# A recurrent attention with two expert layers on one core: low parts of the weights on VectorE, bounded scans, bonus sums on TensorE, and a new order of the slots

## The chip, the core and the metric

The kernel runs on 1 core of one Trainium2 chip. The metric is the device time of one execution in microseconds (us); lower is better.

## The reference

```python
for t in range(S):                                   # B, H, S, D = 4, 8, 768, 48
    cur = np.einsum('bhd,bhe->bhde', u[None] * kt, vt)
    y[:, :, t] = np.einsum('bhd,bhde->bhe', rt, state + cur)
    state = wt[:, :, :, None] * state + np.einsum('bhd,bhe->bhde', kt, vt)
x = y as (B * S, H * D)                              # 3072 tokens, 384 channels
gate = 1 / (1 + exp(-(x @ w_gate)));  val = x @ w_val   # 384 -> 1536
x = gate * val @ w_out                                  # 1536 -> 384
r = max(x @ w_in, 0);  out = (r * r) @ w_out2           # 384 -> 2048 -> 384
```

The decays w lie between 0.80 and 0.95. The weights of the two expert layers come as 64-bit floats, all else as 32-bit floats.

## The kernel before, in words

The attention runs in 24 chunks of 128 tokens (4 sequences, 6 chunks each; four chunks make a group of 512 tokens). The first expert layer is cut into 72 slots: for each of the 6 groups, 12 slots of 128 hidden channels. The second layer follows with 6 groups of 16 slots. Every large product is made of three matmuls (`mm3`: high part by high part, high by low, low by high), so each weight and each activation exists as a rounded high part and a low part, the difference.

The program has one order, written out by hand, and each engine takes its own instructions in that order. `START` is the order of the first two groups; `steady` makes it for the later ones. A letter with a number is a step:

- `L` loads a chunk: `load_att` (r and k with channels on partitions, and the padded decays) and `load_tok` (r, k and v with tokens on partitions). A load that reuses a buffer waits on SyncE's queue until the buffer's readers are done.
- `C` (`st_clamp`) bounds the decays on GpSimd, for chunk 0 in two halves on VectorE. `S` (`st_scan`, chunk 0 in halves `S0` and `s0`) makes the running products of the decays from the right and from the left with two scans, and multiplies r and k by them.
- `B` and `R` make the bonus term, the sum of r, u and k over the channels of a head: `B` two products on GpSimd, `R` a sum on VectorE, and then a select on GpSimd that lays the sums on the diagonals of `am`.
- `A` multiplies k by r on TensorE and puts the part over the diagonal into `am` with two predicated copies on VectorE; `K` transposes k; `Y` makes the chunk's output and splits it into `xh` and `xl`; `U` and `D` update and decay the state; `G` (`st_guard`) counts decays outside the bounds on ScalarE.
- `P` and `Q` are a slot's gate and value projections (27 matmuls of 512 columns make a slot, `M` included), with the sigmoid on ScalarE and the product and its rounding behind them; `l` is the low part of that product on VectorE; `M` multiplies by the third weight matrix, one slot later.
- `T` is a tick of the stream that converts the first layer's weights. One unit of 128x1152 weights takes three ticks on VectorE (`a`, `b`, `c`: L174, L183, L194), and with the next unit's first tick its high part on ScalarE (L245) and its low part on GpSimd, in three instructions (L248). Slot k of group 0 needs unit k. `t` and `r` are the ticks of the second layer's stream and of its refill from a copy in memory. `W` is a series of small matmuls that nothing reads.

Until `Z` the small products take turns in eight PSUM banks, afterwards in three.

Of the kernel before, what the change touches and what calls it, by code (L numbers as in the profile page):

```python
# [5 lines left out]
F32 = mybir.dt.float32  # L6
# [9 lines left out]
DM = H * D  # L16
C = 128
# [30 lines left out]
W_LOW, W_HIGH = 0.74, 1.34  # L48
# [7 lines left out]
CHANNELS = [o + e for o in range(0, DM, 2 * D) for e in (*range(D), *(D + x for x in ODD))]  # L56
VW = 64
# [8 lines left out]
def rwkv_moe(tc, att, tok, vt, u, w1, w2, out):  # L66
# [3 lines left out]
    with ExitStack() as ctx:  # L70
# [6 lines left out]
        ub = sb.tile([128, DM], F32, name="ub")  # L77

# [34 lines left out]
        nc.vector.memset(inj, 0.0)  # L113
# [31 lines left out]
        class Unit:  # L145
# [58 lines left out]
        class Stream:  # L204
# [10 lines left out]
            def tick(self):  # L215
# [4 lines left out]
                if part == 0:  # L220
# [3 lines left out]
                    if k < len(self.u):  # L224
                        self.u[k].a()
# [10 lines left out]
        def w1_unit(f, note=None):  # L236
# [74 lines left out]
        def load_tok(i, **place):  # L311
# [29 lines left out]
        def st_scan(i, p0, p1):  # L341
# [32 lines left out]
        def st_bonus2(i):  # L374
# [3 lines left out]
            nc.vector.reduce_sum(  # L378
# [493 lines left out]
```

## Time and profile before

| | us |
|---|---|
| median of 3 runs (1028.63 to 1030.43) | 1029.77 |
| the profiled execution | 1029.08 |
| its span | 1027.4 |
| TensorE busy in the span | 967.2 |
| VectorE busy | 541.7 |
| ScalarE busy | 363.8 |
| GpSimd busy | 226.6 |

The profiled execution's own time is 1.68 us longer than its span. Busy is the time in which an engine had an instruction under way; PEclk in the rows below is the share of TensorE's full clock that was granted.

### The profile page before, as it was taken

The page shows a single profiled execution, that of the slowest core. Times are in us where ns is not written, and L with a number is a line of the kernel's source. Part 1 is how long each engine was busy: PE and PEld are TensorE (multiplying, and loading weights), DVE is VectorE, ACT ScalarE, POOL GpSimd, SP SyncE. Part 2 cuts the span into 40 slices and gives each one's busy share as a digit, 9 for nine tenths or more (in the row PEclk, how much of TensorE's full clock was granted, in tenths as well). Part 3 has the DMA queues.
Part 4 walks back from the last instruction along what each step waited for, and adds up shares of the span by engine and source line. Part 5 has one row for each costly group of instructions (what it writes and reads, how often), then busy time and mean ns, then how long its engine had stood idle before and what let it go on. Part 6 is the DMA issues. An engine that isn't in the chain of part 4 may idle for free.

```text
span 1027.4 us, 14742 instructions
## 1 busy us (share of the span) xinstructions
PE 967.2 (94%) x6013; PEld 809.0 (79%) x6013; DVE 541.7 (53%) x763; ACT 363.8 (35%) x676; POOL 226.6 (22%) x175
## 2 busy tenths in 40 slices
PE   3489889999999999999998999999999999999996
PEld 2357667877877777777787788999999999999995
DVE  4889985464577777767642323333333334333332
ACT  0466563232333333333323433332333333332322
POOL 4668675223022222222202550000000000000000
PEclk6579999999999999999999999999999999999999
DMA  9826112113433443445303221010010010100000
GB/s 287 293 112 248 43 53 84 54 53 115 152 123 130 138 153 123 135 154 161 110 9 108 92 78 63 1 62 1 1 62 1 10 53 1 62 1 1 31 1 35
DMA packets 29597, 87.05 MB, mean 85 GB/s; under 512 B 3328, under 2 KB 14944, under 8 KB 27984
## 3 DMA queue, kind: packets, MB, share of 16 engines
q1 hardware_dynamic: 29520, 86.02, 25.5%
q8 instruction: 49, 0.80, 0.4%
q14 instruction: 28, 0.23, 0.1%
HBM read 70.28 MB, written 15.73 MB: 84 GB/s over the span
## 4 chain that ended last, share of the span: by engine, by line
PE 71%; DVE 13%; issue 5%; POOL 4%; ACT 3%; DMA 2%; SPq 0%; DVEq 0%; ACTq 0%; POOLq 0%
PE gv L462 10%; PE gv L464 9%; PE gv L463 9%; PE acc L691 5%; PE acc L689 5%; PE acc L690 5%; PE rot L463 3%; PE rot L464 3%; PE rot L462 3%; PE acc L462 3%; PE acc L463 3%; PE acc L464 3%; DVE cum L353 2%; DVE cum L348 2%; DMA a<-in_att 2%
## 5 line engine op out<-in xcount | busy, mean ns | idle before, releaser
L462 PE MATMUL gv<-xh,w 128*128 128x512 f32 x432 | 174.0, 403 | 8.1 <-DVE sig L497 5.2
L464 PE MATMUL gv<-xh,w 128*128 128x512 f32 x432 | 170.9, 396 | 2.8 <-POOL w L248 2.8
L463 PE MATMUL gv<-xl,w 128*128 128x512 f32 x432 | 170.0, 393 | 0.0
L680 DVE TENSOR_TENSOR sig<-sig 128x512 f32<-128x512 f32 x96 | 66.4, 692 | 185.6 <-ACT sig L679 185.6
L462 PEld LDWEIGHTS gv<-xh,w 128*128 128x128 f32 x432 | 81.6, 189 | 32.2 <-DVE sig L497 9.9
L63 DVE TENSOR_TENSOR gl<-sig,gh 128x512 fp32r<-128x512 f32 x96 | 66.5, 693 | 65.9 <-PE rot L691 37.1
L464 PEld LDWEIGHTS gv<-xh,w 128*128 128x128 f32 x432 | 81.4, 189 | 23.3 <-POOL w L248 4.6
L497 DVE TENSOR_TENSOR sig<-gv,sig 128x512 f32<-128x512 f32 x72 | 49.4, 687 | 92.6 <-PE gv L464 80.1
L689 PE MATMUL acc<-w,gh 128*128 128x384 f32 x288 | 97.1, 337 | 0.1
L691 PE MATMUL acc<-w,gl 128*128 128x384 f32 x288 | 97.0, 337 | 0.1
L690 PE MATMUL acc<-w,gh 128*128 128x384 f32 x288 | 96.7, 336 | 0.0
L463 PEld LDWEIGHTS gv<-xl,w 128*128 128x128 f32 x432 | 81.6, 189 | 17.3
L498 ACT CAST gh<-sig 128x512 fp32r<-128x512 f32 x72 | 44.7, 620 | 135.9 <-DVE sig L497 135.9
L387 POOL TENSOR_SCALAR_AFFINE_SELECT am<-a 128x1024 f32<-128x1024 f32 x22 | 28.5, 1297 | 277.3 <-DVE a L378 277.3
L462 PE MATMUL acc<-gh,w 128*128 128x512 f32 x216 | 88.5, 410 | 0.0
L463 PE MATMUL acc<-gl,w 128*128 128x512 f32 x216 | 85.0, 394 | 1.2 <-DVE gl L502 1.0
L62 ACT CAST gh<-sig 128x512 fp32r<-128x512 f32 x96 | 59.6, 621 | 74.0 <-DVE sig L680 74.0
L464 PE MATMUL acc<-gh,w 128*128 128x512 f32 x216 | 84.8, 393 | 0.0
L492 ACT ACTIVATE sig<-gv 128x512 f32<-128x512 f32 x72 | 42.8, 595 | 104.9 <-PE gv L464 103.6
L502 DVE TENSOR_TENSOR gl<-sig,gh 128x512 fp32r<-128x512 f32 x72 | 55.9, 778 | 20.5 <-ACT gh L498 20.5
L679 ACT ACTIVATE sig<-gv 128x512 f32<-128x512 f32 x48 | 28.8, 600 | 102.8 <-PE gv L464 100.8
L679 ACT ACTIVATE sig<-rot 128x512 f32<-128x512 f32 x48 | 28.8, 600 | 93.0 <-PE rot L464 92.6
(124 smaller groups left out, 1878.7 us busy)
## 6 DMA issues: line engine op xcount, KB each, us to landing
a<-in_att SPq DMA_DIRECT2D x23, 675.5 KB, 6.1
t<-in_tok SPq DMA_DIRECT2D x24, 640.0 KB, 6.7
raw<-in_w SPq DMA_DIRECT2D x12, 1152.0 KB, 12.6
raw<-in_w SPq DMA_DIRECT2D x32, 384.0 KB, 4.0
w2f<-h SPq DMA_DIRECT2D x32, 192.0 KB, 2.4
h<-w2f SPq DMA_DIRECT2D x32, 192.0 KB, 2.5
x2d<-x2o SPq DMA_DIRECT2D x18, 256.0 KB, 2.0
x2r<-x2d SPq DMA_DIRECT2D x6, 768.0 KB, 4.6
```

Source lines behind the costliest of these rows:

```text
L62: nc.scalar.copy(hi, src)
L63: nc.vector.tensor_tensor(out=lo, in0=src, in1=hi.bitcast(F32), op=ALU.subtract)
L462: nc.tensor.matmul(o, w_hi, x_hi, start=start, stop=False)
L463: nc.tensor.matmul(o, w_hi, x_lo, start=False, stop=False)
L464: nc.tensor.matmul(o, w_lo, x_hi, start=False, stop=stop)
L497: nc.vector.tensor_tensor(out=self.s[:, :n], in0=gv[1][:, :n], in1=self.s[:, :n], op=ALU.mult)
L502: nc.vector.tensor_tensor(out=self.gl[:, :n], in0=self.s[:, :n], in1=self.gh[:, :n].bitcast(F32), op=ALU.subtract)
L679: nc.scalar.activation(r, self.h, AF.Relu)
L680: nc.vector.tensor_tensor(out=r, in0=r, in1=r, op=ALU.mult)
L689: nc.tensor.matmul(o, self.gh[:, cs], hi, start=b0, stop=False)
L690: nc.tensor.matmul(o, self.gh[:, cs], lo, start=False, stop=False)
L691: nc.tensor.matmul(o, self.gl[:, cs], hi, start=False, stop=b1)
```

## The change

1. A unit's low part is one VectorE instruction of 128x1152 instead of three of 128x384 on GpSimd.
2. There is no clamp of the decays any more. The scans combine a product with a minimum instead of a product with a sum: the running product never passes 2^54, and the padding columns hold 2^100, so that each head pair's scan starts afresh there from what the second operand holds. A small instruction on 4 columns bounds the value ahead of the reciprocal.
3. For the first eight chunks the bonus sums are made of the product r times k with channels on partitions (one VectorE instruction of 112x512, on the raw r and k) by four matmuls with two columns each (`up` holds u), and copied from PSUM by ScalarE; the loads of those chunks' token tiles leave r and k out. The select on GpSimd stays, and so does the whole old way for the later chunks.
4. The first loads come in another order, `START` is a new order, and the later groups follow a pattern of three slots per chunk (`STEADY`). The absolute value that begins a unit of the second layer's stream is issued on ScalarE one tick earlier.

The host lays out the padding and the small tensor `uc`.

```diff
 START = """
-    W19 B0 S0 C1 s0 R0 K0 B1 A0 R1 U0 S1 T C2 T S2 Y0 B2 K2 G0 T L4 G1 R2 C3 A1 A2 K1 T B3 S3 U1 Y1 T U2 R3 L5
-    A3 Y2 C4 T B4 Y3 K3 U3 G3 Z T S4 R4 P0 G4 Q0 K4 P1 T D4 T A4 Q1 C5 U4 T T l0 l1 S5 G2 T P2 Y4 M0 B5 T D5 T
...
+    B0 S0 s0 R0 W19 B1 A0 R1 T K0 U0 S1 T B2 S2 T Y0 G0 T G1 R2 K2 A1 K1 T B3 U1 A2 S3 Y1 R3 L4 U2 Y2 L5 A3 T
+    G3 B4 K3 Y3 U3 T R4 P0 T Q0 S4 Z G4 D4 P1 K4 T l0 A4 B5 U4 T Q1 T l1 T S5 Y4 G2 M0 P2 T T D5 R5 T M1 Q2 P3
+    l2 T K5 G5 Q3 P4 T T A5 M2 l3 T T Q4 L6 B6 T U5 l4 Y5 T P5 T M3 Q5 M4 T S6 l5 P6 T L7 D6 Q6 R6 K6 T P7 l6
+    M5 T A6 T Q7 T M6 T l7 U6 P8 T Q8 T l8 B7 M7 P9 T S7 Y6 G6 T D7 R7 T Q9 L8 A7 P10 K7 M8 T Q10 l9 l10 U7 T
+    G7 Y7 M9 P11 Q11 M10 L9 B8 l11 M11 S8 P12 R8 Q12 P13 K8 B9 D8 l12 A8 Q13 P14 Y8 l13 M12 S9 M13 D9 G8 Q14 T
...
 """
+STEADY = """
+    K t t P B+ D Q A l M t t P t Q G S+ Y l U t M R+ P t L Q t M l t
+"""
...
-W_LOW, W_HIGH = 0.74, 1.34
+MOST = 2.0**54
+AFRESH = 2.0**100
...
+EARLY = 8
...
-        nc.vector.memset(inj, 0.0)
+        nc.vector.memset(inj, MOST)
...
+            def size(self):
+                if wide and self.note is None:
+                    self.h = self.get_h()
+                    nc.scalar.activation(self.h, self.hi.bitcast(F32), AF.Abs)
...
                 if self.note is None:
-                    nc.scalar.activation(h, self.hi.bitcast(F32), AF.Abs)
                     nc.vector.tensor_scalar(out=h, in0=h, scalar1=TINY, scalar2=HUGE, op0=ALU.max, op1=ALU.min)
...
                     self.u[k].c()
+                    if k + 1 < len(self.u):
+                        self.u[k + 1].size()
...
                 w = w_slot(f)
-                nc.scalar.copy(flat(w[:, 0]), h)
-                for n in range(3):
-                    cs = slice(DM * n, DM * n + DM)
-                    nc.gpsimd.tensor_tensor(
-                        out=w[:, 1, n], in0=h[:, cs], in1=w[:, 0, n].bitcast(F32), op=ALU.subtract
-                    )
+                split_hi_lo(nc, flat(w[:, 0]), flat(w[:, 1]), h)
...
-            nc.sync.dma_start(t, tok[chunk[i]["b"], chunk[i]["c"]])
+            z = 2 * DM if i < EARLY else 0
+            nc.sync.dma_start(t[:, z:], tok[chunk[i]["b"], chunk[i]["c"], :, z:])
...
-            if i == 0:
-                st_clamp(i, p0, p1, nc.vector)
             nc.vector.tensor_tensor_scan(
                 out=suf[:, fl][:, ::-1], data0=wz[:, fl][:, ::-1], data1=inj[:, fl][:, ::-1],
-                initial=0.0, op0=ALU.mult, op1=ALU.add,
+                initial=1.0, op0=ALU.mult, op1=ALU.min,
             )
-            nc.vector.reciprocal(out=inj_p[:, sl, 0:1], in_=end_p[:, sl])
+            start = inj_p[:, sl, 0:1]
+            nc.vector.tensor_scalar(out=start, in0=end_p[:, sl], scalar1=1.0 / MOST, scalar2=None, op0=ALU.max)
+            nc.vector.reciprocal(out=start, in_=start)
             nc.vector.tensor_tensor_scan(
-                out=pre[:, fl], data0=wz[:, fl], data1=inj[:, fl], initial=0.0, op0=ALU.mult, op1=ALU.add
+                out=pre[:, fl], data0=wz[:, fl], data1=inj[:, fl], initial=1.0, op0=ALU.mult, op1=ALU.min
             )
...
         def st_bonus(i):
             t = chunk[i]["t"]
+            if i < EARLY:
+                a = chunk[i]["a"]
+                rk = chunk[i]["rk"] = sb.tile([PR, NP, C], F32, name=f"rk{i}", tag="rk", bufs=2)
+                nc.vector.tensor_tensor(out=rk, in0=a[:, :, 0], in1=a[:, :, 1], op=ALU.mult)
+                return
...
+            if i < EARLY:
+                pb = bank()[:, 0:H]
+                for p in range(NP):
+                    nc.tensor.matmul(pb[:, 2 * p : 2 * p + 2], d["rk"][:, p], up[:, p], start=True, stop=True)
+                nc.scalar.copy(a0.rearrange("p (n a) -> p a n", n=2), pb.rearrange("p (a n) -> p a n", n=2))
+            else:
+                nc.vector.reduce_sum(
...
         load_att(0, True)
         load_tok(0)
-        nc.sync.dma_start(ub, u)
-        s1.fetch(1)
+        nc.sync.dma_start(up, uc)
         load_att(1)
         load_tok(1)
-        s1.fetch(2)
+        s1.fetch(1)
         load_att(2, tag=f"w{F1 - 1}")
         load_tok(2, tag=f"w{F1 - 2}")
-        s1.fetch(3)
         load_att(3, tag=f"w{F1 - 3}")
         load_tok(3, tag=f"w{F1 - 4}")
+        s1.fetch(2)
+        nc.sync.dma_start(ub, u)
+        s1.fetch(3)
```

In `steady`, the lists that spread a chunk's steps over slots k-1, k and k+1 (`S` of the next chunk behind `l`, `D` behind `P`, `A` and `K` behind `Q`, `Y` and `U` one slot later, three ticks in every slot) give way to the loop that walks through `STEADY`, where `+` means the next chunk; the last group, which has no attention, keeps its order.

## Rows read from the trace of the kernel before

**Rows 1.** Windows: busy us (instructions) by engine, granted TensorE clock, DMA share, GB/s.

```profile
25.00:57.90 32.90, 17.00 (x205) 13.42 (x205) 27.21 (x30) 12.70 (x26) 22.41 (x14) 0.55 0.82 289
57.90:161.50 103.60, 92.49 (x669) 70.55 (x670) 90.43 (x91) 65.83 (x115) 74.92 (x48) 0.97 0.32 110
161.50:257.00 95.50, 95.44 (x707) 75.81 (x706) 49.17 (x70) 27.79 (x58) 27.83 (x20) 1.00 0.22 69
...
257.00:350.30 93.30, 92.46 (x696) 73.81 (x695) 64.66 (x108) 33.07 (x71) 18.03 (x15) 1.00 0.43 142
350.30:443.70 93.40, 91.32 (x689) 72.45 (x688) 69.33 (x113) 32.11 (x70) 20.88 (x16) 1.00 0.45 141
443.70:537.00 93.30, 89.86 (x619) 70.83 (x619) 62.00 (x96) 29.52 (x63) 16.73 (x13) 1.00 0.31 97
```

**Rows 2.** Timeline of the start: start us, duration us, instruction, idle time before it.

```profile
16.30 1.92 POOL L322 TENSOR_SCALAR a<-a 112x512 f32<-112x512 f32 x1 [5.32 <-DMA a<-in_att]
...
52.68 2.53 PE L435 MATMUL acc<-room,t 128*32 128x128 f32 x32 [3.48 <-DVE room L417]
...
56.77 1.09 PE L449 MATMUL acc<-t,room 128*64 128x48 f32 x16 [0.62 <-ACT room L403]
57.80 0.80 PE L462 MATMUL gv<-xh,w 128*128 128x512 f32 x1
...
160.85 0.60 ACT L492 ACTIVATE sig<-gv 128x512 f32<-128x512 f32 x1 [2.87 <-PE gv L464]
```

**Rows 3.** The page, DMA issues: count, KB each, median us to landing.

```profile
a<-in_att SPq DMA_DIRECT2D x23, 675.5 KB, 6.1
t<-in_tok SPq DMA_DIRECT2D x24, 640.0 KB, 6.7
raw<-in_w SPq DMA_DIRECT2D x12, 1152.0 KB, 12.6
```

**Rows 4.** GpSimd's groups in 0 to 154 us: busy, mean ns, idle before.

```profile
L248 POOL TENSOR_TENSOR w<-h,w 128x384 fp32r<-128x384 f32 x33 | 49.5, 1527 | 23.3 <-ACT w L245 23.3
L322 POOL TENSOR_SCALAR a<-a 112x512 f32<-112x512 f32 x7 | 16.2, 2319 | 6.2 <-DMA a<-in_att 5.7
```

**Rows 5.** VectorE's groups in 57.9 to 161.5 us: busy, mean ns, idle before.

```profile
L194 DVE SCALAR_TENSOR_TENSOR h<-raw,h 128x1152 int32<-128x1152 int32 x10 | 16.9, 1686 | 0.1
L183 DVE SCALAR_TENSOR_TENSOR h<-raw,h 128x1152 int32<-128x1152 int32 x10 | 16.7, 1669 | 0.1
L502 DVE TENSOR_TENSOR gl<-sig,gh 128x512 fp32r<-128x512 f32 x11 | 13.0, 1191 | 2.0 <-ACT gh L498 2.0
...
L348 DVE TENSOR_TENSOR_SCAN cum<-a,inj 112x520 f32<-112x520 f32 x4 | 6.0, 1495 | 0.1
```

**Rows 6.** Timeline, instructions that nothing holds up: VectorE from 131.7 and 303.6 us, ScalarE.

```profile
131.72 0.75 DVE L174 TENSOR_SCALAR h<-raw 128x1152 int32<-128x1152 int32 x1
132.49 0.69 DVE L502 TENSOR_TENSOR gl<-sig,gh 128x512 fp32r<-128x512 f32 x1
133.10 0.35 DVE L456 TENSOR_TENSOR S<-rot,S 112x192 f32<-112x192 f32 x1
133.36 1.35 DVE L183 SCALAR_TENSOR_TENSOR h<-raw,h 128x1152 int32<-128x1152 int32 x1
...
303.62 1.23 DVE L348 TENSOR_TENSOR_SCAN cum<-a,inj 112x520 f32<-112x520 f32 x1
...
307.52 0.55 DVE L183 SCALAR_TENSOR_TENSOR h<-raw,h 128x384 int32<-128x384 int32 x1
...
132.36 1.15 ACT L245 CAST w<-h 128x1152 fp32r<-128x1152 f32 x1
```

**Rows 7.** Timeline: VectorE's scan beside a busy GpSimd, and TensorE's four transposes.

```profile
75.40 2.06 DVE L348 TENSOR_TENSOR_SCAN cum<-a,inj 112x520 f32<-112x520 f32 x1
...
76.33 1.93 POOL L371 TENSOR_TENSOR t<-t 128x384 f32<-128x384 f32 x1
...
87.86 0.55 PE L398 MATMUL rot<-ident,a 112*128 112x112 f32 x4
```

More of the change, by code (lines that the diff above doesn't have):

```diff
@@ L63, in split_hi_lo, with rwkv_moe @@
     nc.vector.tensor_tensor(out=lo, in0=src, in1=hi.bitcast(F32), op=ALU.subtract)
-def rwkv_moe(tc, att, tok, vt, u, w1, w2, out):
+def rwkv_moe(tc, att, tok, vt, u, uc, w1, w2, out):
     nc = tc.nc
@@ L77, in rwkv_moe @@
         ub = sb.tile([128, DM], F32, name="ub")
+        up = sb.tile([PR, NP, 2], F32, name="up")
         state = [sb.tile([PR, NP, D], F32, name=f"S{b}") for b in range(B)]
@@ L608, in steady @@
         def steady(g):
-            work = [[[], [], [], []] for _ in range(F1 + 1)]
-            if g + 1 < NG:
-                n = len(GROUPS[g + 1])
-                for j, i in enumerate(GROUPS[g + 1]):
-                    k = F1 // n * j
-                    if k > 0:
-                        work[k - 1][0] += ["C", i]
-                        work[k - 1][1] += ["B", i]
-                        work[k - 1][2] += ["S", i]
-                        work[k - 1][3] += ["R", i]
-                    work[k][0] += ["D", i]
-                    work[k][1] += ["A", i, "K", i]
-                    work[k][3] += ["G", i]
-                    work[k + 1][1] += ["Y", i]
-                    work[k + 1][2] += ["U", i]
-                    work[k + 1][3] += ["L", i + 2]
-                    if j == n - 1 and i + 1 < len(ORDER):
-                        work[F1 - 1][0] += ["C", i + 1]
-                        work[F1 - 1][1] += ["B", i + 1]
-                        work[F1 - 1][2] += ["S", i + 1]
-                        work[F1 - 1][3] += ["R", i + 1]
+            if g == NG - 1:
+                return last()
@@ new lines, in steady @@
+            seq, n = [], dict(P=F1 * g, Q=F1 * g, l=F1 * g, M=F1 * g - 1)
+            for i in GROUPS[g + 1]:
+                for t in STEADY.split():
+                    if t in n:
+                        seq += [t, n[t]]
+                        n[t] += 1
+                    elif t == "t":
+                        seq += ["t", 0] if g >= NG - 4 else []
+                    elif t == "L":
+                        seq += ["L", i + 2]
+                    elif i + len(t) - 1 < len(ORDER):
+                        seq += [t[0], i + len(t) - 1]
@@ L631, in steady, with last @@
+            return seq
+        def last():
             seq = []
             for f in range(F1):
-                if NG - 4 <= g < NG - 1:
-                    for q in (0, 2, 3):
-                        work[f][q] += ["t", 0]
-                if g == NG - 1 and f:
-                    for q in range(1, 4):
-                        work[f][q] += ["r", 0]
-                if g == NG - 1:
-                    if f == 0:
-                        work[f][2] += ["F", 0]
-                    if f == 6:
-                        work[f][1] += ["x", 0]
@@ L644, in steady @@
-                k = F1 * g + f
-                seq += ["P", k] + work[f][0] + ["Q", k] + work[f][1] + ["l", k] + work[f][2]
-                if k > 0:
-                    seq += ["M", k - 1]
-                seq += work[f][3]
+                k = F1 * (NG - 1) + f
+                r = ["r", 0] if f else []
+                seq += ["P", k, "Q", k] + r + (["x", 0] if f == 6 else []) + ["l", k] + r
+                seq += ["F", 0] if f == 0 else []
+                seq += ["M", k - 1] + r
             return seq
@@ L760, in scan_attention @@
                         nc.vector.scalar_tensor_tensor(
-                            out=pr, in0=vb, scalar=uc, in1=st[:, 0:S], op0=ALU.mult, op1=ALU.add
+                            out=pr, in0=vb, scalar=ue, in1=st[:, 0:S], op0=ALU.mult, op1=ALU.add
                         )
@@ L789, in general @@
             wtile.clear()
+            thirds.clear()
             again = Stream([w1_unit(f) for f in range(F1)], 2)
@@ L840, in lay_out @@
     vt = v.reshape(B, H, S, D).transpose(0, 1, 3, 2).reshape(B, DM, S)
-    u = np.broadcast_to(np.asarray(i["u"]).reshape(1, DM), (128, DM))
+    u = np.asarray(i["u"]).reshape(NP, 2, D)
+    uc = np.zeros((PR, NP, 2), u.dtype)
+    for j in range(2):
+        uc[64 * j : 64 * j + D, :, j] = u[:, j].T
+    u = np.broadcast_to(u.reshape(1, DM), (128, DM))
     def cols(m, f):
```

38 lines of the change are left out of this document (18 added, 20 removed).

## The prediction

> **What bounds the kernel now.** I read the windows first, because the share of busy time over the whole span hides that the kernel has two halves [rows 1]. From 161.5 us on TensorE has 95.44 us of work in 95.5 us, then about 92.5, 91.3 and 89.9 in groups of 93.3 to 93.4 us: it sets the pace, and only about 0.8, 2.1 and 3.4 us of these three groups are idle. Before that it is different. In 25 to 57.9 us TensorE is busy for 17.0 of 32.9 us, at 0.55 of the clock, while VectorE is busy for 27.2 us; in 57.9 to 161.5 us TensorE has 92.5 and VectorE 90.4 us of work in 103.6 us.
>
> The timeline gives the two marks of the start [rows 2]. The first projection P0 begins at 57.80 us, and the sigmoid of slot 11, the last one whose weights are converted on the way, begins at 160.85 us. In between lie 103.05 us. What is behind the second mark is TensorE's own work and moves with it. So the change is worth what it takes from (a) the time to P0, (b) the 103.05 us, (c) the idle rest of the later groups. The first chunk after chunk 0 waits for its data until 16.30 us [rows 2], and in VectorE's groups the same instructions are longer than they have to be [rows 5, 6]: those are the two things that I cost.
>
> **The price of one instruction.** From start to start [rows 6]: a VectorE instruction of 512 columns takes 0.61 us (132.49 to 133.10), one of 1152 columns 1.35 at most by its own time, the first step of a unit 0.77 (131.72 to 132.49), a chunk's scans with reciprocal and product 3.90 (303.62 to 307.52). I scale the smaller ones by 0.61: a predicated pair is 1.22, an `xl` of 384 columns 0.47.
>
> The low part of a unit on VectorE is not in the trace; its nearest row is the 1152-column instruction with two inputs, 1.35 us [rows 6]. Its lower bound is 1.1 (384 columns at 0.47, two more thirds at the same rate less the fixed part), its upper bound the held-up mean of 1.69 [rows 5]. I take 1.35. On GpSimd the same took three of 1.53 us [rows 4].
>
> The scan with a minimum is not in the trace either. The nearest row is the scan with a sum, 1.23 us for the same 520 columns; I take that for both ends, except for the rival below. The bound ahead of the reciprocal works on four columns: between nothing and 0.35 (the 192-column row), I take 0.2. So `S` is 4.1 us. The product of r and k has 512 columns: 0.61. The four bonus matmuls lie between nothing and the four transposes, 0.55 us [rows 7]; I take 0.55. The copy by ScalarE lies behind them where that engine has room (65.8 of 103.6 us busy [rows 1]).
>
> **(a) To P0.** SyncE's loads come in one queue. Before chunk 1's first tile there were 675.5 KB of chunk 0, its 640 and a unit of 1152 [rows 3], and 192 of `ub` (128 x 384 floats); with its own 675.5 that is 3335 KB, landed at 16.3 us [rows 2], or 215 KB per us from the first issue at 0.8. Now chunk 0's token tile is 256 KB (128 x 512 floats), `ub` and the unit come later: 1611 KB, so chunk 1 is there at 8.3 to 10 us, the first unit (3019 KB) at 14.9, chunk 2 at 18, chunk 3 at 22, the second unit (6034 KB) at 28.9. That is a gain for VectorE only if it isn't busy: by its new order it does chunk 0 (0.61 for the product, then the two halves, together about a whole `S`), then `B1`, `A0`, and at 14.9 the first unit.
>
> From there VectorE's queue up to the second copy of `A3` is: 0.77, S1 4.1, b 1.35, B2 0.61, S2 4.1, c 1.35, `xl` 0.47, 0.7 of waiting for the high part (ScalarE's cast of 1.15 less that `xl`), low part 1.35, next unit's first step 0.77, A1 1.22, b 1.35, B3 0.61, A2 1.22, S3 4.1, two `xl` 0.94, 0.8 of waiting for A3's matmuls, A3 1.22. Sum 27.0, so 41.9 us. Then TensorE does Y3 (2.53) and U3 (1.09) [rows 2] and the bonus of chunk 4 (0.55): P0 at 46.1 us instead of 57.80. The first unit's data leave no slack and the second's a microsecond; chunk 4's load starts once chunk 0's tile is read, long before `S4`. I take 46, with 43 to 50 as bounds, and count **11.8 us**.
>
> **(b) From P0 to slot 11.** Two sums. TensorE: the 92.5 us that it has now, and three bonus sums (R5 to R7), 1.65: 94.2. VectorE: the 90.4 us that it has now [rows 1]. From these I take what is held up: L194 and L183, ten each, 0.34 and 0.32 over 1.35; L502, eleven, 0.50 over 0.69; the scans, four, 0.27 over 1.23, and the two lines like it (the other scan and the product, four each); in all 3.4 + 3.2 + 5.5 + 3.2 = 15.3 us [rows 5, 6]. One row shows where that comes from: a scan of 2.06 us while GpSimd has a multiplication, itself of 1.93 us, under way [rows 7]. GpSimd is busy 74.9 us of this stretch [rows 1]; three kinds of its work go (the low parts, 49.5 us in the first 154, the clamps, 16.2 [rows 4], and the bonus products), and one select per chunk is left. I add ten low parts, 13.5, four bounds, 0.8, and three products for four reduces, at most 1.8 and no gain taken. VectorE then has 91 us, about what it has now: its new work is paid for by what no longer holds it up.
>
> So neither engine gets below 94 us, and both wait for each other in order: a slot's projection for the unit's low part, whose path is shorter by 3 x 1.53 less 1.35, and VectorE's product for the projection. Bounds: 94.2 (no waits) and 103.05 (the present waits stay). I take 97.5, nearer to the sum, because the low parts on GpSimd, at the end of every unit's path, go; this gives **5.5 us**.
>
> The Trainium skill ("SBUF — State Buffer", section "SBUF: two separate sides") states that VectorE and GpSimd share one pair of ports as an exclusive lock: a VectorE instruction with two SBUF inputs and a GpSimd instruction that reads SBUF shut each other out for the whole instruction. The rows agree in direction, the scan being 0.83 us longer [rows 6, 7]. By that rule the selects that stay would still hold VectorE: an estimate by it, with up to 1.9 us for each of the four in (b), takes 7.6 us back and leaves the total at 1018; my sum goes by the rows and counts nothing for them.
>
> **(c) The later groups.** At most 0.8 + 2.1 + 3.4 = 6.3 us of idle time are there [rows 1]. The absolute value one tick earlier takes a wait of VectorE away, and the pattern puts the scans of the next chunk ahead of `Y` and `l`, with two thirds of a slot of TensorE's work before `M` needs `l`. I take 1.5 us, bounds from a loss of 4 to a gain of 5. The second layer has no changed instruction.
>
> **Sum.** 11.8 + 5.5 + 1.5 = 18.8. Against the profiled execution's own 1029.08 us that is 1010.3; the median of the runs shown is 0.7 us higher, which I leave out.
>
> **The rivals.**
>
> *Only the start moves.* Stretch (b) keeps its 103 us: VectorE has as much work as now, and the selects that stay, four in this stretch, hold it up by as much as the multiplication of 1.93 us [rows 7], which is 7.6 us against the 5.5 counted. Then 1029.1 - 11.8 = 1017.3, or 1016 with half of (c). For it: 91 and 94 us side by side leave little room for two engines that wait for each other. Against it: the shorter end of each unit. 0.22.
>
> *TensorE is filled.* (b) falls to 94.2 and P0 to 44, (c) gives 4: 13.8 + 8.9 + 4 = 26.7, so 1002.4. For it: the rows after 161.5 us show that TensorE runs without gaps once it is ahead. 0.14.
>
> *The later pattern costs.* The scans, 4.1 us, with `xl` and `l` behind them, come in one piece; if that makes the third slot's product late by 1 us in each of the twelve chunks, 12 us go and 1022 is left. For it: groups four and five already lose 2 to 3 us. 0.05.
>
> *The scan with a minimum is slower.* The place is each `S`: with x us more per scan, VectorE loses 2x in each of eight chunks of the start, where it has no room, and in twelve later ones beyond about 1.6 us of slack. From 16x + 12(2x - 1.6) = 18.8, it decides from x = 0.95, a scan of 2.2 us; at double price (x = 1.23) it is 30 us less the gain, 1040. Nothing in the trace speaks for it, and nothing shows such a scan. 0.04. This is the one that ends slower than before.
>
> *The forecast.* 1006 to 1014. 0.55.
>
> **Numbers.** The likeliest is 1010.3. The range goes to the filled TensorE with a little more, 1000, and past the rival of the start alone and the page's estimate, 1020: it leaves out the last two rivals and the far ends, about 0.15. A measurement of this kernel can tell about 0.2% (2 us) from no change. Faster: all but the slow scan, part of the later pattern's tail and 0.01 for costs that I don't see, 0.93; within 0.2%: 0.02; slower: 0.05.
>
> **What would show it.** P0's first matmul at 43 to 50 us (46) and the sigmoid of slot 11 at 140 to 149 us (143.5); chunk 1's scan on VectorE before the first unit's second step, at 15 to 16 us; twelve low parts of 128x1152 on VectorE at 1.3 to 1.4 us; L183's, L194's and L502's successors near 1.35, 1.35 and 0.69; scans at 1.23; GpSimd busy about 100 us instead of 227; TensorE's idle time in a later group under 3 us. The prediction is wrong if the scans are longer, if the VectorE means stay where they are, if P0 is later than 50 us because a load or the queue of VectorE holds chunk 2 or 3 back, or if TensorE waits for `S`, `l` or a product in every later chunk.

## The result and the profile after

The changed kernel takes 1013.64 us (median of 4 runs, 1012.05 to 1014.01) beside 1030.1 (4 runs, 1028.63 to 1031.1) for the one before: a ratio of 0.9838 [0.9821, 0.9855]. The profiled execution took 1014.01 us, its span 1012.2, so 15.2 us less than the span before. The forecast was 1010.3 in a range of 1000 to 1020. But the parts came out otherwise than the total, as the marks of the two timelines show:

| stretch (us) | before | after | gain | forecast |
|---|---|---|---|---|
| to P0's first matmul | 57.80 | 51.36 | 6.4 | 11.8 |
| from there to the sigmoid of slot 11 | 103.05 | 103.61 | -0.6 | 5.5 |
| to the sigmoid of slot 24 | 98.85 | 98.49 | 0.4 | 0 |
| three later groups (sigmoids of slots 24 to 60) | 279.3 | 269.5 | 9.8 | 1.5 |
| last group (slots 60 to 71) | 71.83 | 73.43 | -1.6 | 0 |
| rest | 416.59 | 415.82 | 0.8 | 0 |

The page after: busy time, share and instructions of each engine, and the granted clock in 40 slices.

```profile
span 1012.2 us, 14801 instructions
PE 975.2 (96%) x6077; PEld 824.1 (81%) x6077; DVE 535.1 (53%) x798; ACT 366.0 (36%) x685; POOL 102.1 (10%) x100
...
PEclk8589999999999999999999999999999999999999
```

GpSimd is at 102.1 us, as forecast. The windows after, cut at the marks (columns as in [rows 1]):

```profile
25.00:51.30 26.30, 22.64 (x228) 18.92 (x228) 22.16 (x28) 15.03 (x34) 2.66 (x2) 0.52 0.90 305
51.36:154.97 103.61, 94.78 (x692) 74.94 (x692) 88.91 (x106) 62.92 (x113) 10.76 (x6) 0.95 0.28 95
154.97:253.46 98.49, 98.49 (x725) 79.13 (x724) 52.34 (x77) 29.73 (x62) 17.10 (x15) 1.00 0.26 80
253.46:346.00 92.54, 92.54 (x699) 74.64 (x698) 68.85 (x122) 34.26 (x73) 10.47 (x10) 1.00 0.44 141
```

In the second row both sums that the prediction made are nearly met, VectorE 88.91 us (forecast 91) and TensorE 94.78 (94.2). Yet the stretch is no shorter: what is left is waiting, and a granted clock of TensorE of 0.95 where it was 0.97. VectorE's groups in 51 to 154 us (busy, mean ns, idle before) are those of [rows 5]:

```profile
L72 DVE TENSOR_TENSOR w<-h,w 128x1152 fp32r<-128x1152 f32 x11 | 14.9, 1355 | 5.7 <-ACT w L71 5.5
L200 DVE SCALAR_TENSOR_TENSOR h<-raw,h 128x1152 int32<-128x1152 int32 x10 | 13.5, 1354 | 0.1
L526 DVE TENSOR_TENSOR gl<-sig,gh 128x512 fp32r<-128x512 f32 x11 | 7.5, 685 | 2.1 <-ACT gh L522 2.0
L359 DVE TENSOR_TENSOR_SCAN cum<-a,inj 112x520 f32<-112x520 f32 x4 | 4.9, 1235 | 0.0
```

Each of these prices is right: low part 1.355, the units' step 1.354 instead of 1.686, the product's low part 0.685 instead of 1.191, the scan with a minimum 1.235. New is the last column of the first row: VectorE now stands in front of the low part until ScalarE has cast the high part, 5.5 us in five waits. TensorE's own waits in the timeline, with the bonus matmuls of the start:

```profile
9.02 1.84 PE L399 MATMUL rot<-up,rk 112*128 112x2 f32 x8 [9.02 <-DMA up<-in_uc]
...
25.63 1.86 PE L399 MATMUL rot<-up,rk 112*128 112x2 f32 x8 [4.64 <-DVE rk L386]
...
51.36 0.48 PE L486 MATMUL gv<-xh,w 128*128 128x512 f32 x1
...
61.06 1.01 PE L422 MATMUL rot<-ident,a 112*128 112x112 f32 x4 [3.32 <-DVE a L369]
...
154.97 0.60 ACT L516 ACTIVATE sig<-gv 128x512 f32<-128x512 f32 x1 [2.40 <-PE gv L488]
...
527.53 0.19 PE L351 MATMUL rot<-ones,tot 128*1 128x1 f32 x2 [2.57 <-DVE tot L349]
```

At 61.06 K4 waits for chunk 4's scans (`S4`), and in the 9 us behind it the clock is down:

```profile
60.00:65.00 5.00, 3.94 (x36) 3.37 (x36) 3.96 (x6) 3.61 (x7) 0.00 (x0) 0.55 0.11 48
65.00:70.00 5.00, 5.00 (x66) 3.92 (x65) 4.82 (x7) 1.23 (x2) 0.00 (x0) 0.76 0.00 0
```

And in the later groups VectorE's waits for the absolute value have gone. Waits (us in total, times, longest), first before, 260 to 540 us, then after, 253 to 530 us:

```profile
DVE h L173 <- ACT h L172: 44.0, 28, 3.8
```

```profile
DVE h L190 <- ACT h L180: 7.5, 7, 1.7
```

### The profile page after: what moved, and what is told of

Read it like the earlier page. It is cut to its first block, busy times and chain, and to the rows that moved or that the text cites. A ratio compares the mean times of both kernels' runs of the same rounds, so it can differ in the third digit from the quotient of the medians.

```text
span 1012.2 us, 14801 instructions
## 1 busy us (share of the span) xinstructions
PE 975.2 (96%) x6077; PEld 824.1 (81%) x6077; DVE 535.1 (53%) x798; ACT 366.0 (36%) x685; POOL 102.1 (10%) x100
## 4 chain that ended last, share of the span: by engine, by line
PE 87%; DVE 7%; ACT 3%; issue 1%; DMA 1%; SPq 0%; ACTq 0%; DVEq 0%
PE gv L486 12%; PE gv L488 12%; PE gv L487 12%; PE acc L701 5%; PE acc L699 5%; PE acc L486 5%; PE acc L700 5%; PE acc L487 4%; PE acc L488 4%; PE rot L487 3%; PE rot L488 3%; PE rot L486 3%; PE rot L438 2%; PE rot L459 2%; PE rot L700 2%; PE rot L701 2%
## 5 line engine op out<-in xcount | busy, mean ns | idle before, releaser
L72 DVE TENSOR_TENSOR gl<-sig,gh 128x512 fp32r<-128x512 f32 x96 | 66.5, 693 | 65.9 <-PE rot L701 37.1
L689 ACT ACTIVATE sig<-rot 128x512 f32<-128x512 f32 x48 | 28.8, 600 | 93.0 <-PE rot L488 92.5
L526 DVE TENSOR_TENSOR gl<-sig,gh 128x512 fp32r<-128x512 f32 x72 | 52.0, 722 | 16.4 <-ACT gh L522 16.3
```

Source lines behind the costliest of these rows:

```text
L72: nc.vector.tensor_tensor(out=lo, in0=src, in1=hi.bitcast(F32), op=ALU.subtract)
L526: nc.vector.tensor_tensor(out=self.gl[:, :n], in0=self.s[:, :n], in1=self.gh[:, :n].bitcast(F32), op=ALU.subtract)
L689: nc.scalar.activation(r, self.h, AF.Relu)
```

## The experiments

Each run was compared with runs of the kernel before made beside it; their medians were 1030.99 us (e1 to e4), 1028.88 (e5 to e8), 1030.67 (e9 to e11) and 1030.16 (e12). The marks are from each run's own timeline: the sigmoids of slots 0 and 11, and the lengths of the three later groups together and of the last one.

| run | median us | ratio to before | slot 0 | slot 11 | between | three groups | last |
|---|---|---|---|---|---|---|---|
| after | 1013.64 | 0.9838 [0.9821, 0.9855] | 53.70 | 154.97 | 101.27 | 269.5 | 73.43 |
| e1, old lists later | 1012.93 | 0.9837 [0.9809, 0.9865] | 50.45 | 151.68 | 101.23 | 271.5 | 71.82 |
| e2, K4 later | 1015.2 | 0.9856 [0.9838, 0.9874] | 50.72 | 154.52 | 103.80 | 269.5 | 73.44 |
| e3, low part later | 1009.16 | 0.9796 [0.9771, 0.9822] | 51.22 | 151.31 | 100.09 | 269.5 | 71.86 |
| e4, W first | 1011.09 | 0.9818 [0.9797, 0.9838] | 50.59 | 153.41 | 102.82 | 269.5 | 71.88 |
| e5, low parts on GpSimd | 1009.28 | 0.9804 [0.9786, 0.9822] | 52.19 | 150.42 | 98.23 | 269.5 | 73.48 |
| e6, K4's wait filled | 1011.34 | 0.982 [0.9802, 0.9839] | 51.33 | 154.77 | 103.44 | 269.3 | 71.88 |
| e7, old lists, old Abs | 1017.48 | 0.9883 [0.986, 0.9905] | 49.20 | 152.02 | 102.82 | 277.4 | 71.79 |
| e8, old lists, clamps | 1012.89 | 0.985 [0.9825, 0.9875] | 50.40 | 151.63 | 101.23 | 272.2 | 71.78 |
| e9, e5 with S4 earlier | 1010.69 | 0.9809 [0.9792, 0.9825] | 49.83 | 150.95 | 101.12 | 269.5 | 73.42 |
| e10, e9 with a new start | 1009.51 | 0.9786 [0.9766, 0.9805] | 50.26 | 151.20 | 100.94 | 269.5 | 73.43 |
| e11, bonus as before | 1016.0 | 0.9858 [0.9841, 0.9875] | 52.94 | 157.49 | 104.55 | 269.5 | 71.88 |
| e12, e3 with the flag later | 1008.55 | 0.979 [0.9773, 0.9806] | 50.66 | 150.61 | 99.95 | 269.5 | 70.65 |

Two things must be kept in mind. With the same START up to P0, slot 0's sigmoid comes anywhere between 49.2 and 53.7 us (e7, after), so a single profile says little of the start within 4 us. And the last group takes 71.8 or 73.4 us whatever the edit up to e11, which is taken up at e12. The lengths in between repeat far better: the three groups take 269.3 to 269.5 us in every run that leaves them alone.

### Where the gain of the later groups comes from: e1, e7, e8

e1 gives the later groups the lists of before (without the clamp):

```diff
-            for i in GROUPS[g + 1]:
-                for t in STEADY.split():
+            work = [[[], [], [], []] for _ in range(F1 + 1)]
+            for j, i in enumerate(GROUPS[g + 1]):
+                k = F1 // n * j
...
+                work[k][1] += ["A", i, "K", i]
```

> The changed kernel with the lists of before in the later groups (next chunk's scans behind l, A and K behind Q, Y and U one slot later), without clamps. Changed kernel: its groups 2, 3 and 4 take 91.3, 90.9 and 87.3 us from first sigmoid to first sigmoid (before: 92.9, 94.5, 92.0), in all 9.8 us less. Theory: the place of the steps does it; then the three groups come back to 279 us and the median is 1021 to 1024 us. Rival: it is what is missing on GpSimd (no clamp holds VectorE up) or the absolute value one tick earlier; then the groups stay near 270 us and the median at 1013 to 1015 us.

The three groups take 271.5 us, 2.0 more than after and 7.8 less than before. So the rival holds, and the new pattern is 2.0 of the 9.8. e7 also takes back the earlier absolute value:

```diff
-                        if k == 0:
-                            self.u[k].size()
+                        self.u[k].size()
...
-                    if k + 1 < len(self.u):
-                        self.u[k + 1].size()
```

> The changed kernel with the later groups' lists of before, and the absolute value of a second-layer unit back in the tick that needs it; no clamps. Before: groups 2 to 4 take 279.3 us, changed 269.5, with the old lists alone 271.5. In the kernel before VectorE waited 44 us in 28 waits for this absolute value, in the old lists with the early one 9. Theory: these waits, not the order of the steps, made VectorE late for the product, and so TensorE; then the three groups take 277 to 279 us and the median is 6 to 7.5 us over that with the old lists (1012.9). Rival: the clamps that hold VectorE up did it; then the groups stay at 271 to 273 us.

277.4 us: 5.9 more than e1, as the theory said; the median is 4.6 us over e1's, less than the 6 to 7.5 expected. VectorE's waits (250 to 530 us) are those of before again. Of the waits of TensorE's weight loads those for the product (3.8 us; before 8.5, in e1 none) are back; those for the scans, 7.5, are 5.8 in e1 too:

```profile
DVE h L190 <- ACT h L180: 44.4, 28, 3.7
...
PEld rot L435 <- DVE a L366: 7.5, 11, 1.8
PEld gv L483 <- DVE sig L518: 3.8, 9, 0.7
```

e8 is e1 with the clamp on GpSimd in the later groups:

```diff
+        def st_clamp(i):
+            wc = chunk[i]["w"].rearrange("p (a c) -> p a c", c=CW)[:, :, 1 : C + 1]
+            nc.gpsimd.tensor_scalar(out=wc, in0=wc, scalar1=0.74, scalar2=1.34, op0=ALU.max, op1=ALU.min)
```

> The changed kernel with the later groups' lists of before and GpSimd's clamps at their old places in these groups (0.74 to 1.34, which changes no decay); the absolute value stays one tick early. Theory as for the run before it: the groups stay at 271 to 273 us, since VectorE's state decay is longer (1.1 us instead of 0.35) but nobody waits for it. Rival: the clamps did it; then they take 276 to 279 us.

272.2 us: 0.7 more than e1. Beside the clamps it is the second step of a unit (384 columns) that takes longer. The groups of VectorE in 250 to 520 us, of e8 and then of e1:

```profile
L200 DVE SCALAR_TENSOR_TENSOR h<-raw,h 128x384 int32<-128x384 int32 x32 | 25.8, 807 | 0.0
```

```profile
L200 DVE SCALAR_TENSOR_TENSOR h<-raw,h 128x384 int32<-128x384 int32 x32 | 17.6, 549 | 0.0
...
L376 DVE TENSOR_TENSOR S<-S,cum 112x192 f32<-112x192 f32 x12 | 13.1, 1093 | 0.0
```

That is 8.2 us of VectorE over 32 instructions, and 0.7 us of time, because VectorE waits there for TensorE anyway (43.9 us in 14 waits in e1, 250 to 530 us). The state's decay, which the expectation puts down to the clamps, is as long in e1, which has none: it runs beside the select, which stays. In after, where the new pattern puts it elsewhere, it is short:

```profile
L376 DVE TENSOR_TENSOR S<-S,cum 112x192 f32<-112x192 f32 x12 | 4.2, 351 | 0.0
```

So of 9.8 us the earlier absolute value is 5.9, the pattern 2.0, and the clamps 1.9 as what is left (279.3 - 277.4, with the late absolute value) or 0.7 (with the early one).

### Why the stretch to slot 11 gained nothing: e2, e6, e3, e5, e9

Two causes stood against each other: TensorE's wait at K4 with the lower clock behind it, or VectorE's waits in front of the low parts. e2 moves K4, A4 and U4 away from the wait:

```diff
-    ... D4 P1 K4 T l0 A4 B5 U4 T Q1 T l1 T S5 Y4 ...
+    ... D4 P1 T l0 B5 T Q1 K4 A4 U4 T l1 T S5 Y4 ...
```

> The changed kernel with K4, A4 and U4 moved behind Q1, nothing else. Theory: TensorE's wait of 3.3 us for chunk 4's scans at K4, 57.7 to 61.1 us, and the slower granted clock behind it (0.55 and 0.76 in the next ten us) are what kept the stretch from P0 to the sigmoid of slot 11 at 103.6 us; then the stretch is 98 to 100 us and the median 1008 to 1011 us. Rival: VectorE's queue sets the stretch (88.9 us busy of 103.6, the rest waits for other engines); then the wait turns up elsewhere, the stretch stays within 1.5 us of 103.6 and the median within 2 us of 1013.6.

It is no shorter: 103.80 us between the sigmoids, after 101.27 (from P0's first matmul 106.14 after 103.61, which is longer than the rival said too). The wait turns up at U4, which needs ScalarE's copy of what the later K4 made, and VectorE's waits for the cast grew. Waits in e2, 48 to 152 us:

```profile
PEld rot L473 <- ACT kt L427: 6.4, 1, 6.4
...
DVE w L72 <- ACT w L71: 7.6, 7, 2.1
```

e6 keeps the order and fills the wait with 26 matmuls that nothing reads (they are work added, not part of the reference):

```diff
-    ... G4 D4 P1 K4 T ...
+    ... G4 D4 P1 w26 K4 T ...
```

> The changed kernel with 26 unread matmuls (about 2.9 us at full clock) ahead of K4 on TensorE, in its wait of 3.3 us for chunk 4's scans. In the changed kernel the granted clock is 0.55 and 0.76 in the ten us behind this wait. Theory: the slow clock costs 3 to 4 us of the stretch from P0 to slot 11; with the wait filled the clock stays near 1, the stretch is 2 to 4 us shorter and the median 1009.5 to 1012. Rival: VectorE sets the stretch, TensorE's slow ten us are hidden behind it; the clock stays near 1 and the stretch within 1 us of 101.3.

The clock is 1.00 where it was 0.55 and 0.76; the stretch as a whole is not shorter (103.44), though the median, 1011.34, lies where the theory had it. Windows of e6:

```profile
60.00:65.00 5.00, 4.64 (x85) 3.74 (x85) 4.59 (x8) 3.23 (x5) 0.00 (x0) 1.00 0.00 0
65.00:70.00 5.00, 5.00 (x39) 4.05 (x28) 5.00 (x6) 3.35 (x6) 0.00 (x0) 1.00 0.75 188
```

This doesn't clear the clock, for it now falls elsewhere. The sigmoids cut the stretch into parts, and five runs have the same steps in it (after, e1, e4, e7, e8), so the parts show what an edit does. A fall here is a few us at about half the clock:

| run | slots 0 to 5 | 5 to 9 | 9 to 11 | the clock falls |
|---|---|---|---|---|
| after, e1, e8 | 48.8 to 48.9 | 32.0 to 32.1 | 20.4 | at K4 and near slot 4 |
| e4, e7 | 48.8 | 32.0 | 22.0 | there and before slot 10 |
| e6 | 47.1 | 32.9 | 23.5 | near slot 7 and before slot 10 |
| e3, e12 | 47.9 to 48.0 | 31.3 | 20.8 | at K4 and near slot 4 |
| e5 | 45.2 | 31.0 | 22.1 | at K4 |
| e9 | 46.5 | 31.0 | 23.6 | at K4, near slot 3 and before slot 10 |
| e10 | 46.3 | 31.0 | 23.6 | at K4 and before slot 10 |

With K4's wait filled and no fall, slots 0 to 5 take 1.8 us less; slots 5 to 11, with two falls that after doesn't have, take 4.0 us more. What one fall costs is seen in e7 and e1, which differ in nothing before slot 11. Both wait 2.2 us for a scan's product at A7; behind it the clock stays at 1.00 in e1 and falls in e7, and slots 9 to 11 are 1.6 us longer there. In e6 it falls behind 1.9 us. Windows of e1, e7 and e6:

```profile
136.00:144.00 8.00, 7.43 (x44) 6.09 (x45) 7.62 (x10) 4.39 (x9) 3.37 (x3) 1.00 0.53 158
```

```profile
136.00:144.00 8.00, 8.00 (x40) 6.54 (x39) 6.41 (x8) 4.92 (x10) 4.25 (x3) 0.79 0.41 122
```

```profile
136.00:144.00 8.00, 7.48 (x30) 6.11 (x31) 7.61 (x10) 3.44 (x8) 3.42 (x3) 0.57 0.52 159
```

So the clock is one of the things that make this stretch long, and a single "between" holds one to three falls. e3 leaves the work and moves the low part behind the first step of the next unit, so that VectorE has 0.75 us to do while ScalarE casts:

```diff
-                        self.u[k - 1].d()
+                        late = self.u[k - 1].d()
...
                         self.u[k].a()
+                    if k and wide and self.u[k - 1].note is not None:
+                        late()
...
-                split_hi_lo(nc, flat(w[:, 0]), flat(w[:, 1]), h)
+                nc.scalar.copy(hi, h)
+                low = lambda: nc.vector.tensor_tensor(out=lo, in0=h, in1=hi.bitcast(F32), op=ALU.subtract)
```

> The changed kernel with each unit's low part on VectorE behind the next unit's first step instead of ahead of it. VectorE waits 5.5 us in five waits for the cast of the high part in the stretch from P0 to slot 11, and 2.0 us before P0. Theory: these in-order waits took the place of GpSimd's low parts and cost the path; with the next unit's first step (0.75 us) put in, about half of them go, the stretch is 1 to 3 us shorter and the median 1010 to 1012.5 us. Rival: TensorE's own waits or the low part coming 0.75 us later eat it; the median stays within 1 us of 1013.6.

The median is 1009.16 us, under the expected range. VectorE's waits for the cast in 48 to 152 us fall from 5.5 to 2.3:

```profile
DVE w L270 <- ACT w L269: 2.3, 3, 1.4
```

The stretch itself is 1.2 us shorter than after's (100.09), with the clock's falls where after has them, and e12, which has the same order, repeats it (99.95); the rest of what separates the two profiles lies in parts that vary without the edit, the start (2.5) and the last group (1.6). e5 puts the low parts back on GpSimd and keeps everything else:

```diff
-                split_hi_lo(nc, flat(w[:, 0]), flat(w[:, 1]), h)
+                nc.scalar.copy(flat(w[:, 0]), h)
+                for n in range(3):
...
+                    nc.gpsimd.tensor_tensor(out=w[:, 1, n], in0=h[:, cs], in1=w[:, 0, n].bitcast(F32), op=ALU.subtract)
```

> The changed kernel with the low parts of the first layer's weights back on GpSimd, in three instructions per unit; all else stays. From P0's sigmoid to that of slot 11 the kernel before took 99.4 us, the changed one 101.3 and, with the old later pattern, 101.2. Theory: VectorE's queue sets this stretch, and the low parts put 15 us of work and 5.5 us of waits for ScalarE's cast into it; then without them the stretch is 3 to 8 us shorter (93 to 98), and the median 1005 to 1010 us. Rival, as I predicted: what VectorE loses to a busy GpSimd (about 15 us before) comes back with it and the low part comes 3 us later; then the stretch is 101 us or longer and the median 1013 us or more.

1009.28 us, where the theory had it, and the shortest stretch of all, 98.23: 3.0 us less than after, but with one fall of the clock fewer. In slots 5 to 9, where the clock is full in both, it gains 1.0 us, as do e9 and e10. The window and the groups of e5:

```profile
49.90:150.42 100.52, 93.13 (x691) 73.98 (x692) 87.24 (x94) 63.16 (x114) 56.00 (x39) 0.97 0.29 97
...
L200 DVE SCALAR_TENSOR_TENSOR h<-raw,h 128x1152 int32<-128x1152 int32 x10 | 16.0, 1598 | 0.1
L531 DVE TENSOR_TENSOR gl<-sig,gh 128x512 fp32r<-128x512 f32 x12 | 11.3, 939 | 1.9 <-ACT gh L527 1.8
```

VectorE has eleven instructions of 1.355 us fewer and is still busy for 87.24 us: the hold-ups are back (1.598 instead of 1.354, 0.939 instead of 0.685). Part 1 of the change thus exchanged hold-ups for work of the same length, as the prediction said, and added waits, as it did not say. The rule on the shared ports that the prediction cites (the Trainium skill, "SBUF — State Buffer", section "SBUF: two separate sides") agrees in direction, here and in e8. Its estimate of 7.6 us for the four selects is too high, and the prediction's nothing too low: of the four in after's stretch one holds a first step of a unit for 0.9 us (1.65 instead of 0.75, at 53.26), two make VectorE wait for them, 0.99 and 0.39 us, and one meets nothing, in all about 2.3 us.

e9 adds to e5 an earlier S4, so that K4 needn't wait:

```diff
-    ... R4 P0 T Q0 S4 Z ...
+    ... R4 P0 T S4 Q0 Z ...
```

> The kernel with the low parts on GpSimd (1009.3 us, 98.2 us from P0's sigmoid to that of slot 11), with chunk 4's scans ahead of slot 0's product on VectorE (S4 before Q0). In that run VectorE waits 6.3 us for TensorE's projections, 3.2 of them for Q0's, and then TensorE 3.3 us for S4's product at K4. Theory: with VectorE no longer the bound, this swap turns both waits into work; the stretch becomes 94.5 to 97 us and the median 1006 to 1008. Rival: the stretch is set by the conversion of the weights further on; the gain at K4 is lost again by slot 11, the stretch stays within 1 us of 98.2 and the median at 1008.5 to 1010.

1010.69 us, 101.12 in the stretch: outside both the theory and the rival. Slots 5 to 9 are as short as e5's; the other parts are longer, with two falls of the clock that e5 doesn't have.

### The start: e4, e10, e11

e4 puts the unread matmuls `W19` ahead of chunk 0, because after's timeline has them waiting behind R0, whose tile `up` lands only at 9.0 us:

```diff
-    B0 S0 s0 R0 W19 B1 A0 R1 T ...
+    W19 B0 S0 s0 R0 B1 A0 R1 T ...
```

> The changed kernel with the 19 unread matmuls back at the very front of TensorE's order, ahead of R0. In the changed kernel R0 waits until 9.0 us for the small tile of u, and the 19 matmuls (4.2 us) stand behind it, so chunk 0's A begins at 14.9 us, its copies on VectorE at 16.7 and the first unit's first step at 18.0. Theory: this makes chunk 1's scans (19.5 us) and all of VectorE's queue late; with the matmuls in front, A0 begins at 11 to 13 us, chunk 1's scans at 17 to 17.5, P0 comes at 49 to 49.5 instead of 51.4 and the median is 1.5 to 2.5 us lower. Rival: the data of the first unit or of chunk 2, or the slow clock of TensorE ahead of P0 (0.50), set P0; it stays within 0.7 us of 51.4, and the median within 1 us.

VectorE is done with chunk 0 at 15.3 us, and then waits for the data of the first unit:

```profile
13.98 1.33 DVE L441 COPY_PREDICATED am<-mask,acc 128x512 f32<-128x512 int32 x2 [0.78 <-PE acc L438]
17.01 0.76 DVE L191 TENSOR_SCALAR h<-raw 128x1152 int32<-128x1152 int32 x1 [1.70 <-DMA raw<-in_w]
```

The data are there at 17.0 us and not at 14.9 as in the prediction. P0 comes at 48.21 us and the median is 2.6 us under after's, but e1, e2, e6 and e8, with after's START, reach P0 at 48.07 to 49.00 too: nothing here is shown to be the edit's. e10 has W first and S1 ahead of that unit's first step (and the two edits of e9):

```diff
-    B0 S0 s0 R0 W19 B1 A0 R1 T K0 U0 S1 T B2 S2 T ...
+    W19 B0 S0 s0 R0 B1 A0 R1 K0 U0 S1 T T B2 S2 T ...
```

> As the run before it (low parts on GpSimd, S4 before Q0), with the unread matmuls first on TensorE and the first unit's first step behind chunk 1's scans instead of ahead of them. With the matmuls first, VectorE had chunk 0's copies done at 15.3 us and then waited until 17.0 for the first unit's data. Theory: VectorE's queue up to P0 is what sets P0, so chunk 1's scans begin at 15.3 instead of 17.3 to 19.5, P0's sigmoid comes at 48 to 50 us (50.4 to 53.7 in the runs so far) and the median is 1 to 2.5 us under the run before it. Rival: the data of chunk 2 and 3 set it; P0's sigmoid stays at 50.4 or later and the median within 1 us.

Chunk 1's scan begins at 15.93 us instead of e9's 16.84, but slot 0 is no earlier (50.26, e9 49.83). The lead is gone at chunk 2's scan, which begins at 23.40 (e9 22.81): the first unit's step was only moved behind, and a small instruction of chunk 1, beside a select, took 0.88 instead of 0.17 us:

```profile
17.19 0.88 DVE L369 TENSOR_SCALAR inj<-cum 112x4 f32<-112x4 f32 x1
...
23.40 1.23 DVE L364 TENSOR_TENSOR_SCAN cum<-a,inj 112x520 f32<-112x520 f32 x1
```

The median is 1.2 us under e9's. One of its four executions took 1920.88 us; it was not profiled, the ratio leaves it out (the median of the other three is 1009.16), and its cause is open.

e11 takes back the bonus sums of the first eight chunks, products on GpSimd and a sum on VectorE again, with the whole token tiles loaded:

```diff
-EARLY = 8
+EARLY = 0
...
-        nc.sync.dma_start(up, uc)
+        nc.sync.dma_start(ub, u)
```

> The changed kernel with the bonus sums of all chunks the old way: products on GpSimd, sum on VectorE, token tiles with r and k (384 KB more for each of eight chunks), and the tile of u loaded third. Order and all else as in the changed kernel. Theory: the smaller loads and the shorter path bring chunk 1 to 3 in earlier; so without them P0's sigmoid, 50.4 to 53.7 us, comes 3 to 7 us later and the median is 1016 to 1021. Rival: the order of the loads alone did it, TensorE's bonus sums at half clock (1.9 us each ahead of P0) cost as much as they save; then P0's sigmoid stays within 2 us and the median at 1012 to 1015.

1016.0 us, at the low end of the theory; slot 0's sigmoid at 52.94 us, inside the range of the unedited START, and slot 11's at 157.49. Beside after (154.97) and the three others whose steps up to slot 11 are the same (e1, e7, e8: 151.6 to 152.0), part 3 is worth 2.5 to 5.9 us there, some of it the clock, which falls three times in e11.

### The best version: e12

After and e2, e5, e9 and e10 have 73.4 us in the last group, the others 71.8. The timeline has a wait of 2.57 us for the flag's sum there, and the granted clock of the 4 us behind it is 0.57 in after and 1.00 in e3 (window of after, then of e3):

```profile
528.00:532.00 4.00, 4.00 (x12) 3.15 (x11) 0.69 (x1) 0.90 (x2) 0.00 (x0) 0.57 0.22 88
```

```profile
524.00:528.00 4.00, 4.00 (x19) 3.28 (x18) 0.84 (x2) 0.73 (x2) 0.00 (x0) 1.00 0.34 130
```

e12 is e3 with the flag's matmul behind `M`:

```diff
-                seq += ["F", 0] if f == 0 else []
                 seq += ["M", k - 1] + r
+                seq += ["F", 0] if f == 0 else []
```

> The kernel with each unit's low part on VectorE behind the next unit's first step (1009.2 us), and in the last group the matmul that sums the flags behind the mix of the slot before (M) instead of ahead of it. In the changed kernel TensorE waits 2.6 us there for VectorE's reduce, and behind it the granted clock is once 0.57 for about 4 us and once 1.00: the last group takes 73.4 us in four runs and 71.9 in the others. Theory: the mix has nothing to wait for and covers the wait; the last group takes 69 to 69.5 us, no clock falls, and the median is 1005 to 1007.5. Rival: the mix takes the wait on, because the low part or a bank isn't ready; the last group stays at 71.9 or more and the median at 1008 or more.

The wait is half as long, the last group takes 70.65 us, between the theory and the rival, and the kernel 1008.55 us (5 runs, 1007.3 to 1009.54), 0.979 [0.9773, 0.9806] of before. It beats both kernels, but is not told apart from e3, e5 and e10, whose intervals it shares:

```profile
524.01 0.19 PE L358 MATMUL rot<-ones,tot 128*1 128x1 f32 x2 [1.29 <-DVE tot L356]
```

## Why the prediction was right in sum and wrong in its parts

That the total came within 3.3 us is luck: (a) and (b) gave 11.5 us less than was counted, (c) 8.3 more.

**(a), mis-sized.** The term was 11.8 us; after's profile has 6.4. Other executions of the same START reach P0 at 46.84 (e7) to 49.00 us (e6), which is 8.8 to 11.0. In after P0 is 5.3 us later than the working's 46.1, and 3.1 of them are there when VectorE takes the first step of the first unit, at 17.98 us instead of 14.9. That step stands behind the copies of A0, A0 behind `W19` and R0, and R0 behind the product of r and k (`B0`) and `up`. The working waits for none of these. By its rate of 215 KB per us chunk 0 would be there at 3.9 us; `B0`, which the new order puts ahead of chunk 0's scans, begins at 6.85 (in e11, without it, the first scan begins at 3.02), and `up`, a few kilobytes, comes at 9.02. The first unit's own data came at 16.0 to 17.3 us where VectorE had to wait for them (e2, e3, e4, e8, e9), but by 14.69 in e7, and there P0 is 0.7 us from the working. Another 1.6 us are two selects, which the working counts as nothing: the first step beside one takes 1.61 instead of 0.75, a product of chunk 3, at 41.89, 1.93 instead of 1.23. After's rows:

```profile
6.85 0.69 DVE L386 TENSOR_TENSOR rk<-a 112x512 f32<-112x512 f32 x1 [5.25 <-DMA a<-in_att]
...
17.98 1.61 DVE L191 TENSOR_SCALAR h<-raw 128x1152 int32<-128x1152 int32 x1
...
17.89 1.09 POOL L411 TENSOR_SCALAR_AFFINE_SELECT room<-a 128x1024 f32<-128x1024 f32 x1 [5.24 <-ACT a L400]
```

The bonus matmuls, taken at 0.55 us per chunk from the transposes, take 1.86 and 1.87 us in after for chunks 2 and 3, at a granted clock of 0.50, and 1.05 for chunks 1 and 4, at 1.00. e11, without part 3, still reaches P0 at 50.45 us, so most of the start's gain is the loads' new order, START and the missing clamp; which of them was not tried apart.

**(b), failed.** VectorE's prices held, and both sums nearly. What failed is "I take 97.5, nearer to the sum, because the low parts on GpSimd, at the end of every unit's path, go". It leaves out three things. The first is what stands behind the low part on VectorE: in (a) the working puts down 0.7 us of waiting for the high part, in (b) it has ten units and none. That wait, 5.5 us in after, is in order, so scans and products queue behind it. e3 and e12 (only the order) got 1.2 to 1.3 us of the stretch back; low parts off VectorE, with the hold-ups back, got 1.0 in slots 5 to 9 alone (e5, e9, e10). The second is TensorE's clock, which stands nowhere in (b): its 94.2 us start from the 92.5 of before, at a clock of 0.97, and after has 0.95. Behind K4's wait it fell to about 0.5, the lower of the two levels (1.2 of 2.4 GHz). Without that fall and the one near slot 4 the first five slots are 1.8 us shorter (e6), and a fall before slot 10, which after doesn't have, costs 1.6 (e7, e4). The third is the selects, put at nothing: about 2.3 us. What these add up to together was not tried in one run, and why the clock falls behind one wait and not behind an equal one stays open.

**(c), far too small.** "At most 6.3 us of idle time are there" was read from busy times, and 9.8 us came out. The rows show why that is no bound. A matmul is shown 0.39 us long, and the next one starts 0.23 us after it:

```profile
345.65 0.39 PE L488 MATMUL gv<-xh,w 128*128 128x512 f32 x1
345.88 0.39 PE L486 MATMUL gv<-xh,w 128*128 128x512 f32 x1
346.11 0.39 PE L487 MATMUL gv<-xl,w 128*128 128x512 f32 x1
```

A stall of up to 0.16 us between two such rows leaves no idle time. The waits of the weight loads do show more; before, 260 to 540 us:

```profile
PEld gv L462 <- DVE sig L497: 8.5, 10, 1.2
PEld rot L414 <- DVE a L356: 5.8, 11, 1.4
```

That is 14.3 us in 21 waits, for the product of a slot and for the scans, both done by a VectorE that itself stood 44.0 us behind the absolute value. With the early one the waits for the product go, and those for the scans, 5.8 us, stay until the pattern changes (e1, after). The step that was named and not priced (the absolute value one tick earlier) is worth 5.9 us, more than all of the later groups were given.

**The rivals.** "Only the start moves" is nearest to what (b) did, though by the cast and the clock more than by the selects. "The later pattern costs" fell: it gains 2.0 (e1). The slower scan fell at 1.235 us. TensorE was not filled.

## What to carry to other kernels

When work moves to an engine that takes its instructions in order, price the wait for its operand as well as its length, and put something between the producer and it (e3). Before a stretch is compared between two runs, compare the granted clock in it part by part: in e6 a filled wait gained 1.8 us in one part and the clock took it back in others. A bound on what a group can gain is not its idle time where the rows of pipelined matmuls overlap; read the waits of the weight loads, and the waits of the engine that feeds them, too. Where a total comes out right, compare it stretch by stretch: here an overestimate of 11.5 us in (a) and (b) met an underestimate of 8.3 in (c).

## What the runs showed of the hardware that was not expected

Four fp32 products with two columns (eight rows of the trace) take 1.86 us at a granted clock of 0.50 (25.63 us in after), nearly as long as the sixteen matmuls of A1 behind them (2.08 us at 30.68, same clock). A tile of a few kilobytes, third in SyncE's queue behind chunk 0's 930 KB, lands at 9.0 us in after and at 7.0 to 7.8 in other executions. A select on GpSimd holds a 112x192 product of VectorE, 1.24 instead of 0.35 us (e1). Behind a wait of 2.57 us of TensorE, after a stretch at full clock, the granted clock was 0.57 in some executions and 1.00 in others, of kernels that are alike there; behind 2.2 us at A7 it was 1.00 in e1 and fell in e7, and behind 3.3 us at K4 it was 0.55.
